# A routed feed-forward layer on one core: the second expert's search is written out earlier, and four weight pieces wait for a gather

## The chip, the core and the metric

The kernel runs on one core of a Trainium2 chip. Its engines work side by side, each through its own queue in order: TensorE (PE in the profile; its weight loads are PEld), VectorE (DVE), ScalarE (ACT), GpSimd (POOL) and SyncE (SP). SP issues the plain DMAs, POOL the indirect ones. The metric is the device time of one execution in microseconds (us). Before the change it was 879.24 us, the median of 3 runs (879.12 to 879.32).

## The reference

A retention layer (4 batches, 8 heads, 576 positions, head width 64) gives 2304 tokens of width 512. A dense feed-forward layer of width 2048 with its own activation follows. The last part is a routed layer over 8 experts:

```
logits = x @ w_gate                      # 2304 x 8
for idx in argsort(-logits.flatten()):   # best pairs first
    tok, e = idx // 8, idx % 8
    if assigned[tok] >= 0 or counts[e] >= 288: continue
    assigned[tok] = e; counts[e] += 1
for e in range(8):
    out[mask_e] = relu(x[mask_e] @ w1[e]) @ w2[e]   # 512 -> 1024 -> 512
```

Every expert takes exactly 288 tokens.

## The kernel before

`first_part` computes the retention layer and the dense layer and leaves the tokens in `ydram` and the logits in `L`. `second_part` does the routing and the experts.

**The search.** The greedy assignment is done in eight phases; each finds the expert that fills next and the logit at which it fills. For phases 0 to 6 the generator `routing_fast` runs three levels. At a level VectorE compares all logits with 63 or 64 thresholds (`reach`, L673), TensorE counts them per expert (18 small products, `cnt`, L955), VectorE marks the full ones (L959), TensorE adds the marks up (`dg`, L965) and VectorE makes the next, finer thresholds (`tau`, L971). After the third level (`de`, L975) a chain of small VectorE operations (L977 to L1004) gives the tokens of the phase (`sel`) and the number of the expert (`EINT`). `slots` (rp, L892) numbers the tokens; `compaction` turns these numbers into an index list `ix` by comparisons on VectorE (`hot`, L851) and 18 products on TensorE (`dv<-cv,hot`, L858). It puts its eight steps into the list `fills`. In the kernel before, `slots` follows at once only for phase 0 and the last two phases; for the others it waits in `pend` until the next phase's first count.

**The experts.** `fetch` issues the 512 KB pieces of an expert's weights on SP (L782), eight for each expert, into four buffers `wraw`; the first piece waits for `EINT`. `split` makes of each piece a rounded half `wxh` (ACT, L792) and a rest `wxl` (POOL or DVE, L794). Pieces 1 to 4 are the first layer, 5 to 8 the second. `gather` fetches the 288 rows by three indirect DMAs on POOL (L1195). `turn` and `transposes` turn them on TensorE (L1201), and ACT (L1214) and DVE (L1218) make the two halves `xth` and `xtl`. `ffn` is 192 products: 96 of the first layer (L1240) and 96 of the second (L1254); after each product it yields. `store` (L1265) turns the result back and scatters it during the next expert's products.

**What sets the order.** The order on each engine is the order in which the program writes it out. `clk` is a planner's clock for each engine, in estimated us. In the loop over an expert's products each product adds `MM` = 0.122 to `clk["pe"]`; between products the loop writes out the next step of the search (`step`, when `clk["route"]` is reached), the next step of a compaction (`fill`), the next expert's gather (as soon as its `ix` is written), a weight split, a store or a block of three turns. The generator's `yield cost, extra` tells how long VectorE is expected to need until the next step. If expert 1's index list is not there when expert 0's products are all written, the code below the loop forces the rest of the search and the gather before expert 1.

In the kernel before, the first count of phase 1 is written after 42 products of expert 0, its `slots` after 151, and its last compaction steps and gather only behind all 192. Expert 2's gather is written after 88 products of expert 1 and its first turns after 121.

**The start.** Ahead of the loop stand the whole search of phase 0, its first four pieces, its gather, one step of phase 1 (the comparisons of its first level, on DVE), the rests of the four pieces on DVE (`los`), the turns of expert 0 and then `fetch()`, which issues pieces 5 to 8; their buffers come free when `los` has read them.

Of the kernel before, what the change touches and what calls it, by code (L numbers as in the profile page):

```python
# [19 lines left out]
N, DM, FF, E, F = 2304, 512, 2048, 8, 1024  # L20
# [707 lines left out]
def second_part(ctx, tc, L, ydram, wx, cst, out, st, fast, L0=None):  # L728
# [5 lines left out]
    nc = tc.nc  # L734
# [38 lines left out]
    def fetch():  # L773

        while len(fetched) < 4 and SRC.get("next", 0) // 8 in EINT:
            n = SRC.get("next", 0)
            ph, i = n // 8, n % 8
            if i == 0:
                r = nc.sync.value_load(EINT[ph], min_val=0, max_val=E - 1)
                SRC[ph] = wx[bass.ds(r, 1)].rearrange("o p f -> p (o f)")  # L780
            raw = wk.tile([P, 1024], F32, tag="wraw", name="wraw", bufs=4)
            nc.sync.dma_start(raw, SRC[ph][:, i * 1024:(i + 1) * 1024])  # L782
            clk["dma"] = max(clk["dma"], clk["pe"] + 2.0) + 1.5
            fetched.append((ph, i, raw, clk["dma"]))
            SRC["next"] = n + 1
# [18 lines left out]
    clk = {"pe": 0.0, "dve": 0.0, "pool": 0.0, "route": 0.0, "dma": 0.0, "gather": 0.0}  # L804
# [3 lines left out]
    def on_dve(cost, ready=0.0):  # L808
        clk["dve"] = max(clk["dve"], clk["pe"], ready) + cost

    def rush(force=False):
        while urgent and (force or urgent[0][0] <= clk["pe"]):
            urgent.pop(0)[1]()
# [71 lines left out]
    def routing_fast():  # L885
# [3 lines left out]
        def slots(ph, sel, rs, dm=None):  # L889

            rp = ps_rt([P, 2], "rp")
            nc.tensor.matmul(rp[:, 0:1], tri, rs, start=True, stop=True, skip_group_check=True)  # L892
            nc.tensor.matmul(rp[:, 1:2], ones, rs, start=False, stop=True, skip_group_check=True)

            def rest():
                rps = rt([P, 2], "rps")
                V.tensor_copy(rps, rp)
                sl = sl_[ph % 2]
                V.tensor_tensor_scan(sl, one18, sel, rps[:, 0:1], op0=ALU.mult, op1=ALU.add)
                slot = rt([P, NT], "slot")  # L900
                V.tensor_mul(slot, sl, sel)
                compaction(ph, slot)

                def check():
                    V.scalar_tensor_tensor(bad, rps[:, 1:2], float(CAP), bad, op0=ALU.not_equal,
                                           op1=ALU.add)
                    if dm is not None:
                        V.scalar_tensor_tensor(bad, dm, 0.5, bad, op0=ALU.is_lt, op1=ALU.add)

                fills.append((None, check))  # L910

            return rest

        pend = None
        for ph in range(E):
# [88 lines left out]
            V.tensor_scalar(ei, em, -1.0, float(E), op0=ALU.mult, op1=ALU.add)  # L1004
            EINT[ph] = ei[0:1, 0:1]
            pend = (ph, sel, rs, dm)
            if ph == 0 or ph >= E - 2:
                yield 2.4, 0.06
                rest, pend = slots(*pend), None
                rest()  # L1010
                yield 1.2, 0.0
# [188 lines left out]
    def turn(tp, ph, k, kt):  # L1200
        nc.tensor.transpose(tp[:, k * 96:(k + 1) * 96], XG[ph][:, k, kt * P:(kt + 1) * P],  # L1201
                            identf[:96, :96])

    def transposes(ph, kt, tp=None):
        if kt == 0:
            XT[ph] = (wk.tile([P, KT, CAP], F32R, tag="xth", name="xth"),
                      wk.tile([P, KT, CAP], F32R, tag="xtl", name="xtl"))
        if tp is None:
            tp = psum.tile([P, CAP], F32, tag="tp", name="tp", bufs=2)
            clk["pe"] += 0.5  # L1210
            for k in range(3):
                turn(tp, ph, k, kt)
        xh, xl = XT[ph]
        nc.scalar.activation(xh[:, kt, :], tp, AF.Copy)  # L1214

        def rest():
            on_dve(0.4)
            V.tensor_sub(xl[:, kt, :], tp, xh[:, kt, :].bitcast(F32))  # L1218

        urgent.append((clk["pe"] + 0.6, rest))  # L1220
# [40 lines left out]
    def store(ph, k):  # L1261
# [21 lines left out]
        scat.append(st)  # L1283

    gen = routing_fast() if fast else routing()
    nxt_pe = [0.0]

    def step():

        clk["pe"] = max(clk["pe"], clk["route"]) + nxt_pe[0]  # L1290
        try:
            cost, nxt_pe[0] = next(gen)
            on_dve(cost, clk["pe"] + 0.25)
            clk["route"] = clk["dve"] + 0.15
        except StopIteration:
            clk["route"] = 1e9

    def pieces(ph, n):
        while len(WSET.get(ph, ())) < n:
            fetch()  # L1300
            split(eng=V if len(WSET.get(ph, ())) % 2 else None)

    while 0 not in EINT:
        step()
    fetch()
    los = [split(True) for i in range(4)]
    while not fills:
# [7 lines left out]
    los[3](V)  # L1315
    tps = [psum.tile([P, CAP], F32, tag=t, name="tp", bufs=b) for t, b in (("tp", 2), ("tp", 2), ("fp", 3), ("fp", 3))]
    for k in range(3):
        for kt in range(KT):
            turn(tps[kt], 0, k, kt)
    for kt in range(KT):  # L1320
        transposes(0, kt, tps[kt])
    rush(True)
    fetch()
    for ph in range(E):
        nxt = ph + 1 < E
# [56 lines left out]
def build(tc, ap, out):  # L1382
    nc = tc.nc
    with ExitStack() as ctx:
        pp = ctx.enter_context(tc.tile_pool(name="pp", bufs=1))
        dp = ctx.enter_context(tc.tile_pool(name="dp", bufs=1, space=bass.MemoryType.DRAM))
        cp = ctx.enter_context(tc.tile_pool(name="cp", bufs=1))
        ctx.enter_context(tc.manual_schedule())
        L = pp.tile([P, NT, E], F32, name="L")
        ydram = dp.tile([N, DM], F32, name="ydram")  # L1390
        cst = {}
        start = []
        cs = ExitStack()

        def begin():
            start.append(Search(cs, tc, L, cst))
            return start[0].early()

        with ExitStack() as c1:
            first_part(c1, tc, ap["att"], ap["att_ht"], ap["att_hn"], ap["dtab"], ap["qtab"],  # L1400
                       ap["ktab"], ap["stab"], ap["wi"], ap["wo"], ap["wgb"], ydram, L, lambda: constants(cp, tc, ap, cst), cst, begin, lambda *a: Grid(cs, tc, L, cst).pieces(*a))
        keep = ctx.enter_context(tc.tile_pool(name="keep", bufs=1, reuse_waits="tile"))
        L0 = keep.tile([P, NT, E], F32, name="L0")
        nc.gpsimd.tensor_copy(L0, L)
        with ExitStack() as c2:
            flag = second_part(c2, tc, L, ydram, ap["wx"], cst, out, start[0], True, L0)
            again = nc.values_load(flag[0:1, 0:1], min_val=0, max_val=1)
        cs.close()
        with tc.If(again != 0):
            with ExitStack() as c3:  # L1410
                general_constants(c3, tc, ap, cst)
                second_part(c3, tc, L0, ydram, ap["wx"], cst, out, Start(c3, tc, L0, cst), False)
# [91 lines left out]
```

## Time and profile before

| What | Number |
|---|---|
| median of 3 runs | 879.24 us |
| the profiled execution's own time | 882.06 us |
| its span, first to last instruction | 880.3 us |
| TensorE busy | 792.0 us, 90% of the span |
| VectorE busy | 574.8 us, 65% |
| POOL busy | 470.5 us, 53% |
| mean granted clock of TensorE | 0.942 |

A granted clock of 0.50 is TensorE's lower level, 1.2 GHz, and 1.00 the upper, 2.4 GHz. Times in rows count from the start of the span. A row of the timeline is: start, duration of the merged instructions, engine, line, operation, what is written from what, how many, and in brackets the idle time of the engine before it with what ended it.

### The profile page before, as it was taken

The numbers are of one execution on the slowest core, as the hardware profiler recorded it, in microseconds if no ns is written. First come the engines' busy times: TensorE is split into PE (matmuls) and PEld (weight loads), VectorE is DVE, ScalarE is ACT, GpSimd is POOL, SyncE is SP. The second block draws the span as 40 slices with busy tenths as digits, with TensorE's granted clock in tenths as the row PEclk, the third lists the DMA queues.
The fourth block names the chain that finished last, engine by engine and source line by source line (L and its number), as shares of the span: only waits on it lengthen the run. The fifth ranks groups of instructions, "written<-read, shape, count | busy, mean of one in ns | idle before, by whom it ended". The sixth has DMA issues, their size and how long they took to land.

```text
span 880.3 us, 16265 instructions
## 1 busy us (share of the span) xinstructions
PE 792.0 (90%) x6151; PEld 720.7 (82%) x6151; DVE 574.8 (65%) x1346; ACT 415.1 (47%) x891; POOL 470.5 (53%) x538
## 2 busy tenths in 40 slices
PE   6687788899999999999999989739699999999994
PEld 6676676788998889888888879629688899999993
DVE  4999999955555688797988955664656635532210
ACT  2454666654544454555455545223244444544621
POOL 3432222265544667566676645214367878778911
PEclk9798989999999999999999999859789999999997
DMA  8535343101204210211100000060546656556401
GB/s 315 178 110 173 125 128 119 50 25 49 68 29 144 73 49 25 96 49 42 65 16 25 2 25 1 25 218 1 172 147 184 181 175 196 149 161 209 124 29 31
DMA packets 27320, 87.63 MB, mean 100 GB/s; under 512 B 4448, under 2 KB 5600, under 8 KB 27104
## 3 DMA queue, kind: packets, MB, share of 16 engines
q1 hardware_dynamic: 24160, 77.06, 27.4%
q0 software_dynamic: 3072, 9.44, 3.3%
q8 instruction: 50, 0.82, 0.4%
q14 instruction: 38, 0.31, 0.1%
HBM read 77.05 MB, written 9.44 MB: 98 GB/s over the span
## 4 chain that ended last, share of the span: by engine, by line
PE 66%; DVE 20%; issue 6%; POOL 2%; DMA 2%; ACT 2%; SPq 0%; DVEq 0%; POOLq 0%; ACTq 0%
PE ph L311 19%; PE hp L1240 9%; PE op L1254 8%; PE b_E L398 8%; PE b_F L398 7%; DVE u L329 3%; DVE raw L162 2%; PE cnt L955 2%; DVE y L167 2%; PE b_A L218 1%; DVE raw L158 1%; DVE u L333 1%; DVE u L324 1%; DVE hot L851 1%; DMA xg<-ydram,ix 1%
## 5 line engine op out<-in xcount | busy, mean ns | idle before, releaser
L311 PE MATMUL ph<-xh,winh 128*128 128x256 f32 x576 | 166.5, 289 | 17.2 <-DVE u L339 11.8
L794 POOL TENSOR_TENSOR wxl<-wraw,wxh 128x1024 fp32r<-128x1024 f32 x58 | 137.6, 2394 | 56.5 <-ACT wxh L792 56.2
L311 PE MATMUL ph<-xl,winh 128*128 128x256 f32 x576 | 164.3, 285 | 0.0
L311 PE MATMUL ph<-xh,winl 128*128 128x256 f32 x576 | 164.2, 285 | 0.0
L329 DVE RECIPROCAL u<-u 128x128 f32<-128x128 f32 x144 | 137.0, 951 | 3.9
L346 POOL TENSOR_TENSOR gl<-u,gh 128x256 fp32r<-128x256 f32 x114 | 86.0, 754 | 93.5 <-ACT gh L345 92.7
L311 PEld LDWEIGHTS ph<-xh,winh 128*128 128x128 f32 x576 | 111.3, 193 | 28.8 <-DVE u L339 16.9
L320 ACT ACTIVATE d<-ph 128x256 f32<-128x256 f32 x144 | 54.9, 381 | 146.9 <-PE ph L311 130.2
L311 PEld LDWEIGHTS ph<-xh,winl 128*128 128x128 f32 x576 | 112.1, 195 | 4.9
L311 PEld LDWEIGHTS ph<-xl,winh 128*128 128x128 f32 x576 | 112.3, 195 | 0.2 <-DVE xl L254 0.2
L324 DVE TENSOR_TENSOR u<-d 128x128 f32<-128x128 f32 x144 | 56.4, 392 | 64.9 <-ACT d L322 59.5
L333 POOL TENSOR_TENSOR u<-d,u 128x128 f32<-128x128 f32 x112 | 52.4, 468 | 53.4 <-DVE u L329 53.3
L792 ACT ACTIVATE wxh<-wraw 128x1024 fp32r<-128x1024 f32 x64 | 67.0, 1052 | 20.1 <-DMA wraw<-in_wx_dram 20.1
L321 ACT ACTIVATE d<-d,half_b 128x256 f32<-128x256 f32 x144 | 73.4, 510 | 4.7
L334 POOL TENSOR_TENSOR u<-d,u 128x128 f32<-128x128 f32 x112 | 68.2, 609 | 8.8
L345 ACT ACTIVATE gh<-u 128x256 fp32r<-128x256 f32 x144 | 58.3, 405 | 17.4 <-DVE u L339 16.9
L322 ACT ACTIVATE d<-d 128x256 f32<-128x256 f32 x144 | 60.2, 418 | 4.5
L1231 DVE SCALAR_TENSOR_TENSOR htl<-hp,hth 128x288 fp32r<-128x288 f32 x64 | 28.7, 455 | 49.8 <-ACT hth L1243 46.8
L355 DVE SCALAR_TENSOR_TENSOR scr<-y,WG 128x512 bf16<-128x512 f32 x64 | 55.3, 864 | 0.4
L339 DVE SCALAR_TENSOR_TENSOR u<-u,ph 128x256 f32<-128x256 f32 x144 | 54.1, 376 | 0.3
L1240 PE MATMUL hp<-xth,wxh 128*128 128x288 f32 x256 | 51.8, 315 | 2.2 <-ACT wxh L792 1.2
L1243 ACT ACTIVATE hth<-hp 128x288 fp32r<-128x288 f32 x64 | 26.1, 408 | 54.5 <-PE hp L1240 48.9
(264 smaller groups left out, 1878.4 us busy)
## 6 DMA issues: line engine op xcount, KB each, us to landing
wraw<-in_wx_dram SPq DMA_DIRECT2D x64, 512.0 KB, 4.2
att<-in_att_dram SPq DMA_DIRECT2D x32, 512.0 KB, 5.4
raw<-in_wi_dram SPq DMA_DIRECT2D x16, 512.0 KB, 3.2
raw<-in_wo_dram SPq DMA_DIRECT2D x16, 512.0 KB, 3.4
ydram<-y SPq DMA_DIRECT2D x9, 512.0 KB, 2.8
WG<-in_wgb_dram SPq DMA_DIRECT2D x1, 2048.0 KB
att<-in_att_ht_dram SPq DMA_DIRECT2D x4, 256.0 KB, 3.7
att<-in_att_hn_dram SPq DMA_DIRECT2D x4, 256.0 KB, 4.2
```

Source lines behind the costliest of these rows:

```text
L311: nc.tensor.matmul(ph, w[f][:, kt, :], x[:, kt, :], start=(k == 0), stop=(k == 11))
L321: nc.scalar.activation(df, df, AF.Square, bias=half_b, scale=-0.5)
L324: nc.vector.tensor_mul(u[:, 0, :], d[:, 0, :], d[:, 1, :])
L329: nc.vector.reciprocal(r, r)
L333: eng.tensor_mul(u[:, 1, :], d[:, 0, :], u[:, 0, :])
L334: eng.tensor_mul(u[:, 0, :], d[:, 1, :], u[:, 0, :])
L346: eng.tensor_sub(gl, g, gh.bitcast(F32))
L398: nc.tensor.matmul(py[n][t], g[:, t * P:(t + 1) * P], w[f], start=(f == 0 and w is woh and g is gh), stop=(f == NF - 1 and g is gl))
L792: nc.scalar.activation(hi, raw, AF.Copy)
L794: rest = lambda eng: eng.tensor_sub(lo, raw, hi.bitcast(F32))
L1240: nc.tensor.matmul(hp, W[kt][w][:, s], x[:, kt, :], start=(k == 0), stop=(k == 11))
L1254: nc.tensor.matmul(op, W[4 + ft // 2][w][:, s], h[:, ft, :], start=(k == 0), stop=(k == 23))
```

## The change

Four edits. The fifth piece of all (`n == 4`) gets a one-column write on POOL ahead of its DMA, so that the DMA waits for POOL's queue, in which the first gather stands. Phase 1's `slots` follows at once, as phase 0's does. A `step()` (the counts of phase 1's first level) is written between the second and the third gathered block of expert 0's turns. A second `step()` (`dg`, `tau` and the comparisons of the second level) stands ahead of `fetch()`, and before it the planner's TensorE clock is set to VectorE's where that is later.

```diff
@@ -779,6 +779,9 @@
             raw = wk.tile([P, 1024], F32, tag="wraw", name="wraw", bufs=4)
+            if n == 4:
+
+                nc.gpsimd.memset(raw[:, 0:1], 0.0)
             nc.sync.dma_start(raw, SRC[ph][:, i * 1024:(i + 1) * 1024])
@@ -1004,7 +1007,7 @@
-            if ph == 0 or ph >= E - 2:
+            if ph < 2 or ph >= E - 2:
                 yield 2.4, 0.06
                 rest, pend = slots(*pend), None
                 rest()
@@ -1315,11 +1318,15 @@
     for k in range(3):
+        if k == 2:
+            step()
         for kt in range(KT):
             turn(tps[kt], 0, k, kt)
     for kt in range(KT):
         transposes(0, kt, tps[kt])
     rush(True)
+    clk["pe"] = max(clk["pe"], clk["dve"])
+    step()
     fetch()
```

## Rows read from the trace of the kernel before

**Rows 1.** Windows: busy us (instructions) of each engine, granted clock, DMA share, GB/s.

```profile
564.90:591.60 26.70, 8.20 (x89) 6.85 (x88) 17.19 (x52) 5.16 (x8) 3.47 (x3) 0.53 0.59 197
591.60:624.80 33.20, 33.18 (x274) 31.55 (x274) 17.66 (x59) 11.26 (x21) 13.06 (x6) 0.91 0.20 68
624.80:636.40 11.60, 5.88 (x68) 4.71 (x69) 8.12 (x31) 1.36 (x4) 3.92 (x4) 0.64 0.44 138
636.40:645.20 8.80, 7.26 (x28) 6.17 (x27) 3.92 (x4) 3.93 (x6) 3.81 (x2) 0.50 0.36 118
645.20:679.00 33.80, 32.21 (x290) 30.29 (x289) 21.20 (x74) 15.95 (x26) 24.89 (x18) 0.95 0.56 163
679.00:711.90 32.90, 31.08 (x289) 29.15 (x288) 18.63 (x64) 16.77 (x27) 28.39 (x20) 1.00 0.64 191
```

**Rows 2.** Page, part 6: the weight pieces' DMAs, count, size, median us from issue to landing.

```profile
wraw<-in_wx_dram SPq DMA_DIRECT2D x64, 512.0 KB, 4.2
```

**Rows 3.** Timeline, 581 to 593 us: the first gather, its turns, expert 0's first products.

```profile
581.02 1.63 POOL L1195 DMA_INDIRECT xg<-ydram,ix  x1 [16.60 <-DVE dv L908]
...
584.05 0.74 DVE L673 TENSOR_TENSOR ind<-dv,g_G 128x567 bf16<-128x567 f32 x1
584.18 0.92 POOL L1195 DMA_INDIRECT xg<-ydram,ix  x1 [0.30 <-issue]
...
586.27 0.87 PE L1201 MATMUL tp<-c_ident,xg 96*128 96x96 f32 x4 [6.53 <-DMA xg<-ydram,ix]
589.69 0.90 PE L1201 MATMUL tp<-c_ident,xg 96*128 96x96 f32 x4 [2.55 <-DMA xg<-ydram,ix]
590.76 0.90 PE L1201 MATMUL tp<-c_ident,xg 96*128 96x96 f32 x4 [0.17 <-DMA xg<-ydram,ix]
...
591.68 1.52 PE L1240 MATMUL hp<-xth,wxh 128*128 128x288 f32 x4
```

**Rows 4.** Windows: the four us in which the second and third blocks land.

```profile
586.00:590.00 4.00, 1.18 (x6) 0.92 (x7) 1.06 (x1) 0.00 (x0) 0.00 (x0) 0.50 0.99 291
```

**Rows 5.** Timeline, 630 to 635 us: the last block of expert 1's gather and its turns.

```profile
630.91 0.92 POOL L1195 DMA_INDIRECT xg<-ydram,ix  x1 [0.30 <-issue]
...
634.00 0.90 PE L1201 MATMUL tp<-c_ident,xg 96*128 96x96 f32 x4 [0.87 <-DMA xg<-ydram,ix]
```

**Rows 6.** Timeline, 637 to 642 us: expert 1's third and fourth weight pieces.

```profile
637.05 1.99 ACT L792 ACTIVATE wxh<-wraw 128x1024 fp32r<-128x1024 f32 x2
```

**Rows 7.** Timeline, 658 to 666 us: expert 2's gather and its first turns.

```profile
658.87 0.94 POOL L1195 DMA_INDIRECT xg<-ydram,ix  x1 [3.75 <-PE cnt L955]
...
665.27 0.30 PE L1201 MATMUL tp<-c_ident,xg 96*128 96x96 f32 x1 [1.08 <-DMA xg<-ydram,ix]
```

**Rows 8.** Windows: two stretches of products at the lower clock.

```profile
591.60:597.30 5.70, 5.68 (x23) 5.57 (x23) 2.01 (x5) 1.35 (x5) 0.00 (x0) 0.50 0.03 11
...
665.60:669.10 3.50, 3.36 (x14) 3.07 (x15) 2.08 (x12) 1.36 (x2) 2.86 (x2) 0.51 0.72 193
```

**Rows 9.** Timeline: products at the upper clock, a count, compaction products, a block of turns.

```profile
598.12 0.69 PE L1240 MATMUL hp<-xtl,wxh 128*128 128x288 f32 x4
598.64 0.69 PE L1240 MATMUL hp<-xth,wxl 128*128 128x288 f32 x4
...
600.07 0.75 PE L955 MATMUL cnt<-oh,ind 128*63 128x8 bf16 x18
...
656.00 0.39 PE L858 MATMUL dv<-cv,hot 128*96 128x6 bf16 x6 [0.35 <-DVE hot L851]
656.25 0.65 PE L1240 MATMUL hp<-xth,wxl 128*128 128x288 f32 x3
...
677.29 0.41 PE L1201 MATMUL tp<-c_ident,xg 96*128 96x96 f32 x3
677.49 0.65 PE L1254 MATMUL op<-hth,wxl 128*128 128x288 f32 x3
```

**Rows 10.** Timeline: a one-element write on POOL.

```profile
646.05 0.09 POOL L1277 MEMSET spacer<- 1x1 f32 x1
```

## The prediction

> **What bounds the kernel now.** I read the page's shares first: TensorE is busy 90% of the span, the next engine 65%, so what counts is where TensorE waits or runs slowly. Then I read the timeline from the end of the dense layer on, cut it into stretches by what TensorE does, and took busy time, granted clock and DMA for each from the windows [rows 1]. Five things are to be seen there:
>
> - From 564.9 to 591.6 us TensorE is busy 8.2 of 26.7 us: the search and compaction of phase 0 and the first gather, one after the other.
> - Expert 0 (591.6 to 624.8) has TensorE busy 33.18 of 33.20 us. Inside it nothing is waited for.
> - From 624.8 to 636.4 no product of an expert runs. TensorE is busy 5.9 of 11.6 us, with the last compaction steps of phase 1, expert 1's gather, and the search of phase 2. POOL and DMA are far from full.
> - Expert 1 takes 8.8 us at the lower clock for its first 22 products, then 33.8 us.
> - Expert 2, with the same kind of work between its products, takes 32.9 us, all at the upper clock.
>
> So the end is set by TensorE's order, and what can be won is the hole between experts 0 and 1 with the slow restart behind it, about 11.6 + 42.6 - 33 = 21 us, and a little at the first gather. Everything from expert 2 on is full: 31.1 of 32.9 us busy.
>
> **The pieces held back.** The first gather's last block leaves POOL at 584.18 + 0.92 = 585.10, and its turns start at 590.76, 5.66 us later [rows 3]. For expert 1 the same step is 631.83 to 634.00, 2.17 us [rows 5]. Between 586 and 590 all DMA engines are busy (0.99, 291 GB/s) [rows 4], and the only other traffic is pieces 5 to 8. With them behind POOL's third issue, block 3 can be there at 585.10 + 2.17 = 587.3, block 1 at 582.65 + 2.17 = 584.8, block 2 between them at about 586.0. The bounds are this (a gain of 3.5 us at the gather) and no gain, if the pieces still collide. I take the first: the pieces' DMAs leave SP about 585.3, and a piece takes 4.2 us to land [rows 2], while 512 KB at 291 GB/s [rows 4] are 1.8 us, so most of it passes before its bytes move.
>
> The write itself is 0.09 us [rows 10], at most the 0.92 us of an indirect issue; POOL has nothing behind it until expert 0's products run. On SP the three later pieces queue behind it and nothing else does. Piece 5 then lands at about 589.5; it is first read after 28 products, at about 595. That cover would have to shrink by 5 us to cost anything.
>
> **The first extra step.** The counts now stand on TensorE between the turns of blocks 2 and 3. Their comparisons are done at 584.79 [rows 3], so they start when block 2's turns end, at 586.0 + 0.9 = 586.9. At the upper clock a count takes at most 0.75 us [rows 9]; here, at the lower, twice 0.7, so 1.4: until 588.3. Block 3's turns, queued behind, start 1.0 us later than the data allow. The first product came 0.92 us after them [rows 3]; with `dg` in front of it I put 589.4. Gain 2.3 us; if the gather is no faster, a loss of 0.2 from `dg`. The second step's VectorE work (2 us) stands behind the four halves of `xtl` and ahead of the first rest of `ffn`, which frees one of three result buffers; no product waits for that before the fourth tile.
>
> **Where phase 1's steps go.** The planner's sums give the order. The step sets TensorE's clock to 23.52; four rests of 0.4 put VectorE at 25.52, to which the new line lifts TensorE; the second step makes that 25.57 and the next step due at 25.57 + 0.25 + 2.0 + 0.15 = 27.97. At 0.122 a product that is after 20 products. Carried on, the second count comes after 20 products, the third after 44, `EINT` after 49, `slots` after 72, compaction from 85, and expert 1's gather after 119; its turns after 161, 170, 179 and 189, and its first four weight splits after 137, 157, 167 and 178. So all that filled the hole is written before expert 0's products end.
>
> Expert 0, from its 33.2 us: one count and its `dg` leave (0.9) and one pair from phase 2 enters (0.9), together nothing. Three sets of compaction products at 0.25 each [rows 9] are +0.75, with waits for `hot` like the 0.35 there, +0.5. Four blocks of turns at 0.2 [rows 9] are +0.8. Gather 1 has 42 products at 0.13 [rows 9] and a count before its first turn, 6.2 us; it needs 0.8 to start, as expert 2's did, two issues of 1.24, then 0.92 + 2.17, so 6.4: +0.2. The lower clock lasted 5.7 us here [rows 8]; TensorE is now busy from 586.0 instead of 589.7 on, so it may rise up to 1.4 us earlier into the products, worth up to 0.7: -0.4. Sum 33.2 + 1.85 = 35.05; expert 1 starts at 624.5 instead of 636.4. Its weights: POOL, free of the gather 4.5 us after its start, needs four rests of 2.4 us and ends 14.1 us after it; TensorE wants the fourth 12.5 + 1.4 us after it. They meet.
>
> Expert 1, from 8.8 + 33.8 = 42.6 us: its first 22 products fall from 8.8 to 22 x 0.13 + 0.4 for the store = 3.3, -5.5. That holds the slow clock and the late splits [rows 6], both gone. Gather 2 stalled TensorE by 1.08 [rows 7], and the clock then fell: 14 products took 3.5 us instead of 1.8 [rows 8]. The stall came with a weight piece in flight; that split now comes earlier, to POOL, and POOL's order keeps the next piece behind the gather. It gets 31 products and two counts, 5.6 us, of the 6.4 it needs: 0.7 stays, without a fall (expert 2 idles 1.8 us at clock 1.00 [rows 1]); -2.1. The third count of phase 2, with `de`, moves in from the hole: +0.9. Sum 35.9; expert 2 starts at 660.4 instead of 679.0. From there the same work follows in nearly the same order, and from expert 3 on in the identical one.
>
> So the profiled execution would fall by 18.6 us, from 882.06 to 863.5. It lies 2.8 us above the median of the runs, so the forecast is 879.24 - 18.6 = **860.6 us**; 857.5 to 863 with the small waits at zero or doubled.
>
> **Rivals.**
>
> *The pieces still collide.* The new wait is for POOL's queue, not for the gather's data: block 3's issue ends 5.66 us before its turns [rows 3]. If the fifth piece starts as soon as POOL is free and takes the engines, block 3 lands as before. The first product then comes at 591.9, 2.5 us later than forecast: 863.1. For it speaks that the data trail the issue by 2.17 us even when little else moves [rows 5]; against it, that a piece's own start takes about as long. The Trainium skill ("Perfetto Trace Analysis", DMA Instruction — SWDGE (GPSIMD)) says that such an instruction's end in the profile is the end of descriptor generation and not of the data movement. The rows agree, 5.66 and 2.17 us; by that rule alone the sum would be this rival's.
>
> *The wait moves to the restart.* VectorE lags the planner, expert 1's gather or its third and fourth splits come late, TensorE stalls at the first turns, and the clock falls as for expert 2: 1.1 + 1.7 [rows 7, 8], and some 1.5 for late splits as at 637 [rows 6]. That is 4.3 us: 865. Against it, gather 1 has nine products more of room than gather 2 had.
>
> *Slower.* The counts now come 20 to 49 products into expert 0, while the clock is still low. If TensorE waits at them so often that the clock does not rise, each product costs 5.7/23 = 0.25 instead of 0.13. The whole gain is used up after 18.6/0.12 = 155 such products beyond the 23; with the other 169 of expert 0 it is 880.5. Against it: four counts stood in expert 0 before with 0.02 us of idle time [rows 1].
>
> *It doesn't do what it says.* VectorE is so late that TensorE waits in the loop for phase 1's index list as long as it did behind it: 879.
>
> **How the numbers follow.** Forecast 0.72, collision 0.14, late restart 0.09, no effect 0.02, slower 0.03. The range takes in the first two and most of the third: 857.5 to 866.0. A measurement of this kernel tells 0.2% (1.8 us) from no change; faster by more 0.95, within 0.02, slower 0.03.
>
> **What would show it.** Block 3's turns near 588.3 and expert 0's first product near 589.4; turns of expert 1 inside expert 0's products; no hole at 624; granted clock 1.00 from about 594 to the end of expert 2; expert 2's first product near 660. The forecast is wrong if TensorE idles over 2 us inside expert 0, or if the clock falls again before expert 2.

## The result, and the profile after

The changed kernel takes **863.63 us** (median; 862.65 to 863.90 in four executions), against 879.26 (879.12 to 879.32) for the kernel before in the same comparison: ratio 0.982 [0.9803, 0.9837], 15.6 us less. The forecast was 860.6 with a range of 857.5 to 866.0 and a gain of 18.6 us. The profiled execution of the changed kernel took 863.57 us (span 861.8); the sum made on the profile had put it at 863.5. Among the runs below, one execution of the kernel with slots as before took 990.51 us at a mean clock of 0.732 and is left out of that kernel's numbers.

Windows of the kernel after: bounds, length, then busy us (instructions) of TensorE, its weight loads, VectorE, ScalarE and POOL, granted clock, DMA share, GB/s. The stretches answer to [rows 1]: search and first gather, the first products of expert 0 at the lower clock, experts 0, 1 and 2.

```profile
564.90:589.20 24.30, 9.46 (x111) 8.05 (x108) 17.59 (x57) 5.58 (x8) 3.58 (x4) 0.54 0.49 162
589.20:594.40 5.20, 5.20 (x22) 4.98 (x21) 3.80 (x9) 1.29 (x4) 0.00 (x0) 0.52 0.72 269
589.20:624.40 35.20, 35.15 (x303) 33.33 (x303) 21.63 (x71) 14.35 (x26) 21.04 (x11) 0.93 0.47 149
624.40:660.90 36.50, 35.49 (x336) 33.28 (x335) 23.60 (x86) 17.48 (x30) 29.79 (x20) 1.00 0.61 180
660.90:694.80 33.90, 31.86 (x296) 30.18 (x296) 20.63 (x72) 17.41 (x30) 28.34 (x20) 1.00 0.61 186
```

There is no stretch without products between experts 0 and 1 any more: in [rows 1] 11.6 us lay there with TensorE busy 5.88. TensorE has 303 instructions in expert 0 where it had 274, and is idle for 0.05 us of it. Expert 1 starts at the upper clock.

The first gather in the timeline of the kernel after (start, busy us, engine, line, operation; in brackets what was waited for), which answers to [rows 3]:

```profile
584.54 0.92 POOL L1198 DMA_INDIRECT xg<-ydram,ix  x1 [0.30 <-issue]
585.26 0.87 PE L1204 MATMUL tp<-c_ident,xg 96*128 96x96 f32 x4 [5.17 <-DMA xg<-ydram,ix]
585.46 0.11 POOL L784 MEMSET wraw<- 128x1 f32 x1
...
586.42 0.90 PE L1204 MATMUL tp<-c_ident,xg 96*128 96x96 f32 x4 [0.29 <-DMA xg<-ydram,ix]
...
587.25 1.12 PE L958 MATMUL cnt<-oh,ind 128*63 128x8 bf16 x18
588.30 0.90 PE L1204 MATMUL tp<-c_ident,xg 96*128 96x96 f32 x4
...
589.14 0.18 PE L968 MATMUL dg<-cl,c_ones 63*128 63x1 bf16 x1
589.25 1.49 PE L1243 MATMUL hp<-xth,wxh 128*128 128x288 f32 x4
```

The third block's turns start 2.84 us after its issue ends (584.54 + 0.92 = 585.46) and wait for no DMA; before it was 5.66 with waits of 6.53, 2.55 and 0.17 ahead of the three blocks. The 18 products of the count stand ahead of the last block, as the sum had them; they took 1.12 us and not 1.4.

The starts of experts 1 and 2 in the same timeline, with the gathers that feed them; they answer to [rows 5] and [rows 7]:

```profile
612.22 0.93 POOL L1198 DMA_INDIRECT xg<-ydram,ix  x1 [3.87 <-PE op L1257]
...
617.50 0.61 PE L1204 MATMUL tp<-c_ident,xg 96*128 96x96 f32 x3
...
624.39 0.69 PE L1243 MATMUL hp<-xth,wxh 128*128 128x288 f32 x4
...
645.10 0.95 POOL L1198 DMA_INDIRECT xg<-ydram,ix  x1 [3.36 <-PE cnt L958]
...
650.64 0.30 PE L1204 MATMUL tp<-c_ident,xg 96*128 96x96 f32 x1 [0.18 <-DMA xg<-ydram,ix]
...
660.86 0.70 PE L1243 MATMUL hp<-xth,wxh 128*128 128x288 f32 x4
```

Expert 1's gather is issued 12 us before expert 0 ends, and its turns wait for nothing. Expert 2's stall is 0.18 us where it was 1.08.

### The profile page after: what moved, and what is told of

Read it like the earlier page. It is cut to its first block, busy times and chain, and to the rows that moved or that the text cites. A ratio compares the mean times of both kernels' runs of the same rounds, so it can differ in the third digit from the quotient of the medians.

```text
span 861.8 us, 16271 instructions
## 1 busy us (share of the span) xinstructions
PE 785.4 (91%) x6151; PEld 716.2 (83%) x6151; DVE 570.8 (66%) x1344; ACT 414.3 (48%) x891; POOL 475.5 (55%) x541
## 4 chain that ended last, share of the span: by engine, by line
PE 68%; DVE 19%; issue 6%; POOL 2%; ACT 2%; DMA 2%; SPq 0%; DVEq 0%; POOLq 0%; ACTq 0%
PE ph L311 19%; PE hp L1243 9%; PE op L1257 8%; PE b_E L398 8%; PE b_F L398 7%; DVE u L329 3%; DVE raw L162 2%; PE cnt L958 2%; DVE y L167 2%; PE b_A L218 1%; DVE raw L158 1%; DVE u L324 1%; DVE u L333 1%; PE b_E L433 1%; DVE gl L346 1%
## 5 line engine op out<-in xcount | busy, mean ns | idle before, releaser
L797 POOL TENSOR_TENSOR wxl<-wraw,wxh 128x1024 fp32r<-128x1024 f32 x60 | 142.4, 2396 | 30.9 <-ACT wxh L795 30.5
```

What stands on the lines that cost most here:

```text
L797: rest = lambda eng: eng.tensor_sub(lo, raw, hi.bitcast(F32))
```

## The experiments

The dense layer does not end at the same time in every execution (561.9 to 564.5 us in these records). So that only the changed part is compared, the table counts from the start of the dense layer's last copy to expert 0's, 1's and 2's first product and to the end of the span, in the one profiled execution of each kernel. The last column is the median of all executions, less the median of the kernel before in the same comparison. That one moves by itself: it was 879.26 beside the changed kernel, 880.03 beside its own repeat, no hold, slots at once and hold; 878.35 beside slots as before, no estimate line, the count behind block 3 and the first unread products; 880.27 beside the last two and the repeat of the changed kernel. So entries of one comparison can be set against each other, and entries of different ones only to about 2 us. The profiled execution is the slowest of its kernel for slots as before (870.71) and for the first unread products (868.03).

```
                              expert 0  expert 1  expert 2     end | medians
before                           29.77     74.50    117.11  318.39 |
kernel before, repeated          29.20     72.60    113.14  314.54 |  +0.5
changed kernel                   26.97     62.11     98.58  299.52 | -15.6
changed kernel, repeated         26.75     61.16     97.66  298.15 | -15.8
changed, no hold                 29.89     64.45    100.99  301.48 | -13.4
before + slots at once           28.90     68.53    113.35  316.88 |  +2.0
before + hold                    26.38     70.49    110.55  311.49 |  -1.7
changed, slots as before         26.93     67.86    107.55  304.74 | -11.4
changed, no estimate line        26.97     62.88     99.61  299.26 | -13.8
changed, count after block 3     27.53     63.28    100.00  298.85 | -14.4
changed + unread products        26.25     60.91    101.65  301.73 | -15.6
changed + more of them           28.75     66.20    102.75  303.11 | -11.5
the same, gather 2 later         29.18     66.14    102.24  303.12 | -14.1
```

**The two kernels again.** No edit; twelve more executions of the kernel before and five of the changed one.

> The kernel before, unchanged. Theory A: the profiled execution of before stood 2.8 us above its other runs because its second gather came late and the clock then fell (1.1 us of waiting, 1.7 us of slow products); an execution near 879.3 us shows the stretch 645.2 to 679.0 some 2.5 to 3 us shorter, with a granted clock of 1.00 in it. Rival B: that fall is in every execution and the 2.8 us lie elsewhere (first part, or the profiler's own cost); then a profile shows the same dip behind 665 us whatever its time.

> The changed kernel, unchanged, beside the two below and with more executions of before. Theory A (the forecast's base, the one profiled execution of before, was 2.9 us above an ordinary one in the part that the change touches): 15 to 16 us below the median of before, and, counted from the end of the dense layer, expert 0, 1 and 2 start within 0.7 us of the first profile of the changed kernel (27.0, 62.1, 98.6). Rival B: the changed kernel varies as before did, and its starts spread by 2 us or more.

Measured: the kernel before 880.54 (877.02 to 887.09, 12 executions; ratio to its own other executions 1.0013 [0.9993, 1.0033]); the changed kernel 864.52 (863.00 to 865.71), ratio 0.9823 [0.9802, 0.9843], again 15.75 us less. The starts of this second record lie within 0.2, 0.95 and 0.92 us of the first record, the latter two a little outside what was expected. The repeated record of the kernel before is the informative one. Its windows, with stretches like those of [rows 1] and expert 0's first 3.1 us on a line of their own:

```profile
591.00:594.10 3.10, 3.08 (x14) 3.00 (x14) 1.55 (x4) 0.91 (x4) 0.00 (x0) 0.54 0.08 32
591.00:622.90 31.90, 31.88 (x274) 30.28 (x274) 17.67 (x59) 11.24 (x21) 12.78 (x6) 0.96 0.20 70
622.90:634.40 11.50, 5.62 (x68) 4.44 (x69) 8.15 (x31) 1.33 (x4) 4.21 (x4) 0.72 0.47 142
634.40:643.10 8.70, 7.16 (x43) 6.07 (x42) 3.92 (x4) 4.46 (x7) 3.66 (x2) 0.59 0.35 120
643.10:675.00 31.90, 30.21 (x280) 28.49 (x277) 21.22 (x74) 15.48 (x26) 25.09 (x18) 1.00 0.60 175
675.00:708.90 33.90, 31.96 (x297) 30.21 (x296) 19.04 (x65) 17.61 (x29) 29.51 (x20) 1.00 0.63 189
```

The hole is the same, 11.5 us against 11.6 [rows 1]. But expert 0's clock rises after some 3 us instead of 5.7 [rows 8]; the first 8.7 us of expert 1 hold 43 instructions of TensorE at clock 0.59 where the 8.8 us of [rows 1] hold 28 at 0.50, so the clock rises earlier there too; and the rest of expert 1 runs at 1.00 throughout, 31.9 us instead of 33.8 (2.5 to 3 us less had been expected), although its stall is there:

```profile
662.63 0.30 PE L1201 MATMUL tp<-c_ident,xg 96*128 96x96 f32 x1 [1.17 <-DMA xg<-ydram,ix]
```

So the profile on which the sum was made holds 1.3 us in expert 0 and 2.1 us in expert 1 (42.6 against 40.5) that another execution of the same kernel does not have, and the stretches differ in the granted clock. The timed executions fit this: of 49 executions that stood beside the kernels below, six took over 882.06 us, and their mean clock was 0.939 to 0.941, near the 0.942 of the profiled one; the eleven of at most 878.2 us had 0.945 to 0.949.

**No hold.** The changed kernel without

```diff
-            if n == 4:
-
-                nc.gpsimd.memset(raw[:, 0:1], 0.0)
```

> The changed kernel without the one-column write, so that pieces 5 to 8 start as before. Theory A (the pieces delayed the first gather): block 3's turns near 590.8 instead of 588.3, expert 0's first product near 591.9, 2.5 us more than the changed kernel: about 866. Rival B (the first gather is slow by itself, the pieces don't matter): the same as the changed kernel, 863.6.

Measured 866.59 (865.02 to 868.61), 0.9847 [0.9822, 0.9872]: 3.0 us above the changed kernel's 863.63, or 2.2 by the last column of the table. The timeline of this run:

```profile
586.54 0.92 POOL L1195 DMA_INDIRECT xg<-ydram,ix  x1 [0.30 <-issue]
...
591.48 0.90 PE L1201 MATMUL tp<-c_ident,xg 96*128 96x96 f32 x4 [1.88 <-DMA xg<-ydram,ix]
```

Here the second block waits 1.88 us and starts 4.0 us behind the end of the third's issue; with the hold it started 0.96 behind. Everything after the first product is as in the changed kernel (34.56 us from expert 0 to expert 1, against 35.14 and 34.41). At the first product the hold is worth 2.9 us (3.1 against the repeat of the changed kernel) and by the medians 2 to 3 us, all at the gather.

**Hold alone.** The kernel before with those two lines.

> The kernel before with the one-column write alone. Theory A: block 3's turns at 587.3 instead of 590.8, and the whole rest moves by that: 3 to 3.5 us less than before, 876. Rival B (the gather is slow by itself): 879.3.

Measured 878.29 (876.36 to 883.02), 0.9983 [0.9965, 1.0001]. By the medians that is 1.7 us where 3 to 3.5 had been expected, and the interval reaches 1: not a difference by itself. Counted from the dense layer's end the first product comes 2.8 us earlier than in the repeat of the kernel before, and the end 3.1 us earlier. In its timeline the third block is clean, since no count stands ahead of it:

```profile
586.04 0.92 POOL L1198 DMA_INDIRECT xg<-ydram,ix  x1 [0.30 <-issue]
...
589.27 0.90 PE L1204 MATMUL tp<-c_ident,xg 96*128 96x96 f32 x4 [0.44 <-DMA xg<-ydram,ix]
590.19 1.52 PE L1243 MATMUL hp<-xth,wxh 128*128 128x288 f32 x4
```

The turns start 589.27 - 586.96 = 2.31 us behind the issue's end, where the forecast took 2.17 and the kernel before had 5.66 [rows 3].

**Slots at once alone.** The kernel before with

```diff
-            if ph == 0 or ph >= E - 2:
+            if ph < 2 or ph >= E - 2:
```

> The kernel before with the second phase's slots at once, and nothing else. By the planner's sums gather 1 is then written after 168 products of expert 0, and all of its turns behind product 192. Theory A: of the 6.4 us that the gather needs, 24 products and the rest cover 3.2; the hole of 11.6 us shrinks to 3 to 4 us, expert 0 starts as in before (591.7): 868 to 870, 872 if the clock falls in the hole. Rival B (the search, not the place of slots, makes the hole): within 2 us of before.

Measured 882.05 (876.97 to 884.03), 1.0021 [1.0002, 1.004]. A plain miss: no gain where 10 us and more had been expected. Its windows (experts 0 and 1, each to the next one's first product):

```profile
592.70:632.30 39.60, 35.31 (x281) 32.89 (x282) 17.87 (x58) 12.54 (x24) 17.01 (x9) 0.89 0.29 90
632.30:677.10 44.80, 41.02 (x351) 37.07 (x350) 23.91 (x75) 17.65 (x30) 26.71 (x18) 0.88 0.41 131
```

And its timeline:

```profile
624.28 0.92 POOL L1195 DMA_INDIRECT xg<-ydram,ix  x1
...
628.80 0.91 PE L1201 MATMUL tp<-c_ident,xg 96*128 96x96 f32 x2 [3.05 <-DMA xg<-ydram,ix]
...
632.35 0.83 PE L1240 MATMUL hp<-xth,wxh 128*128 128x288 f32 x2
...
669.33 0.95 POOL L1195 DMA_INDIRECT xg<-ydram,ix  x1 [4.61 <-PE cnt L955]
...
674.54 0.96 PE L1201 MATMUL tp<-c_ident,xg 96*128 96x96 f32 x5 [0.51 <-DMA xg<-ydram,ix]
...
678.69 1.16 PE L1240 MATMUL hp<-xtl,wxh 128*128 128x288 f32 x4
```

The hole between experts 0 and 1 shrinks (39.6 us from start to start instead of 43.4 in the repeat of the kernel before), but the next search is written later: expert 2's gather goes out at 669 us, 37 us into expert 1 where it was 22.5 before (658.87 [rows 7] less 636.4 [rows 1]), its turns come behind expert 1's last products, and expert 2 starts at the lower clock (1.16 us for four products where 0.7 is usual). Expert 1 takes 44.8 us, against 42.6 and 40.5 in the two records of the kernel before. The hole is handed on to the next expert.

**Slots as before.** The changed kernel with the old condition, `ph == 0 or ph >= E - 2`: hold, estimate and early steps alone.

> The changed kernel with the second phase's slots left for the next phase's first count, as before; the two earlier steps and the held pieces stay. By the planner's sums gather 1 is then written after 150 products of expert 0 (119 in the changed kernel, behind 192 in before) and its first turns after 181. Theory A (what matters is how many products lie between a gather and its turns; the earlier steps alone pull it inside expert 0): 31 products and two counts are 5.6 us of the 6.4 needed, expert 1 starts 1 us later than in the changed kernel, 864 to 865.5. Rival B (slots at once closes the hole): the hole comes back, 870 or more.

Measured 866.97 (866.24 to 870.71, five executions), ratio 0.9859 [0.9835, 0.9882]: 3.3 us above the changed kernel's 863.63, or 4.2 by the last column, between the two theories. The timeline of this run at expert 1's start, in its slowest execution:

```profile
621.31 0.93 POOL L1198 DMA_INDIRECT xg<-ydram,ix  x1 [3.65 <-PE cnt L958]
...
630.60 0.81 DVE L1221 TENSOR_TENSOR xtl<-tp,xth 128x288 fp32r<-128x288 f32 x2
631.09 1.22 PE L1204 MATMUL tp<-c_ident,xg 96*128 96x96 f32 x6 [2.12 <-DVE xtl L1221]
632.02 1.40 PE L1243 MATMUL hp<-xth,wxh 128*128 128x288 f32 x4
```

And its windows there:

```profile
630.00:635.00 5.00, 3.91 (x18) 3.83 (x19) 2.32 (x6) 1.77 (x3) 3.31 (x2) 0.58 0.67 204
635.00:640.00 5.00, 5.00 (x37) 4.50 (x35) 1.04 (x6) 0.61 (x2) 1.18 (x2) 0.50 0.41 126
```

Gather 1 is issued 9 us later than in the changed kernel (7 counted from the dense layer's end), its last turns fall behind expert 0's products, TensorE waits 2.12 us for VectorE there, and the clock goes to 0.50. That is the forecast's second rival, the wait moved to the restart, at its place and at about its price of 4.3 us; in the changed kernel the early slots keep it away. The hold and the early steps without the early slots still keep 11.4 of the 15.6 us.

**Estimate and place of the count.** Two pieces taken out of the changed kernel, one in each run:

```diff
-    clk["pe"] = max(clk["pe"], clk["dve"])
```

```diff
-        if k == 2:
-            step()
```

> The changed kernel without the line that lifts the planner's TensorE clock to VectorE's. The second count then comes after 30 products instead of 20 and gather 1 after 126 instead of 119, its turns after 168. Theory A: everything still lies inside expert 0, within 1 us of the changed kernel, 863 to 864.6. Rival B (the spacing is what makes it): VectorE is still the late one at 20 products in the changed kernel, so ten products more save waits, or the later gather costs 2 us or more: outside 862 to 866.

> The changed kernel without the step between the second and third gathered block; the first level's counts stand behind all turns, ahead of expert 0's first product. Theory A: block 3's turns move up from 588.3 to the landing at 587.5, the counts (1.1 us at the lower clock) then stand ahead of the first product, which moves from 589.25 to 589.5: within 0.7 us of the changed kernel. Rival B (the counts fill TensorE's wait and bring the upper clock forward): 1.5 us or more above it, 865.2.

Measured 864.55 (863.59 to 864.65), 0.9825 [0.9803, 0.9847], and 863.94 (862.54 to 864.66), 0.9821 [0.9798, 0.9843]. Neither differs from the changed kernel by more than its own two medians, 863.63 and 864.52, do; the last column, 13.8 and 14.4 us, cannot tell them from it either. Without the extra step the timeline shows the third block at 589.09:

```profile
589.09 0.90 PE L1204 MATMUL tp<-c_ident,xg 96*128 96x96 f32 x4 [0.51 <-DMA xg<-ydram,ix]
```

That is 3.28 us behind the start of its issue, against 3.76 in the changed kernel: the count holds the last turns up by 0.5 us, and spares as much afterwards (expert 0 starts at 26.97 us in the changed kernel and at 27.53 without the step). No run has the early steps alone, or hold and slots without any early step; what the steps give is known only as the difference between the changed kernel and the parts above.

**Filling the gaps with unread products.** To raise the clock before expert 0, the changed kernel gets products that nobody reads (`warm(n)` writes n of them, 128x128 by 128): in the first run 7 behind the products of `slots` and 14 behind those of the compaction, in the second more of them, from the search on.

```diff
     while not fills:
         step()
+    warm(7)
     fill(True)
+    warm(14)
```

> The changed kernel with products that nobody reads in TensorE's two waits ahead of expert 0: 7 of 128x128 by 128 float32 behind the rp products and 14 behind the compaction products (some 0.42 us each at the lower clock). Theory A (expert 0's first 20 products pay for the idle time ahead of them): the clock is up when block 1 lands, the counts and turns take half, and the first 20 products 0.13 instead of 0.25 us: 2.5 to 3.5 us less than the changed kernel, 860 to 861. Rival B: the clock does not rise in these waits or falls again at once, and expert 0 starts at the lower clock: 863.6, or up to 1 us more where the products run past the landing.

> The changed kernel with unread float32 products (128x128 by 128) in every wait of TensorE during the search of phase 0 and the first gather: 3 behind each dg, 7 behind de, 13 behind rp, 20 behind the compaction products. Theory A (an idle TensorE ahead of expert 0 costs the lower clock in the counts, the turns and the first 20 products): if they hold the upper clock that expert 1 to 7 have, each count on the way takes 0.7 instead of 1.3 us and expert 0's first 20 products 2.6 instead of 5 us: 3 to 4.5 us below the changed kernel, 859 to 860.5. Rival B (as when 21 such products in two waits raised the clock only near the end and it fell again): the unread products run at the lower clock, 0.42 us each, and stand in the way of the counts: 863 to 866.

> The same, and the planner takes gather 2 to need 1 us more, so that expert 2's first turns come after 142 of expert 1's products instead of 134. Theory A (the stall at expert 2's first turns and the fall of the clock behind it come in some executions and cost up to 3 us there): the median is 0.2 to 1 us below the kernel with unread products alone, and no profile shows the lower clock inside expert 1. Rival B: the turns, now 15 products apart, wait for VectorE instead; the same or up to 1 us more.

The third run is the second with 1 us more for gather 2 in the planner's estimate, so that expert 2's turns are written later. Measured: 862.80 (861.10 to 868.03), 0.9803 [0.9781, 0.9825], 0.8 below the changed kernel, within the spread and not below it in the last column; 868.80 (866.97 to 869.47), 0.987 [0.9846, 0.9894]; 866.21 (863.31 to 867.47), 0.983 [0.9805, 0.9854]. Windows of the first of them around expert 0's start, in its slowest execution:

```profile
590.00:592.00 2.00, 1.85 (x9) 1.41 (x10) 1.30 (x4) 1.32 (x4) 0.00 (x0) 0.81 1.02 342
592.00:594.00 2.00, 2.00 (x10) 2.00 (x10) 1.97 (x5) 0.00 (x0) 0.00 (x0) 0.50 0.97 385
```

And of the second:

```profile
580.00:585.00 5.00, 4.70 (x49) 4.70 (x49) 4.08 (x10) 3.23 (x4) 2.45 (x2) 1.00 0.52 193
585.00:590.00 5.00, 2.30 (x31) 1.72 (x29) 3.41 (x7) 0.00 (x0) 1.14 (x3) 1.00 0.76 226
590.00:595.00 5.00, 4.82 (x24) 4.58 (x25) 3.58 (x9) 1.73 (x5) 0.00 (x0) 0.66 0.78 297
```

The unread products do bring TensorE to its upper level, but it does not stay there: in both runs it falls to the lower one just as expert 0's products begin. In the second TensorE was busy for only 2.30 of the 5 us before. There the third block is late as well, and inside expert 0 a turn of expert 1 waits, as the timeline shows:

```profile
585.41 0.92 POOL L1210 DMA_INDIRECT xg<-ydram,ix  x1 [0.31 <-issue]
...
590.03 0.55 PE L1216 MATMUL tp<-c_ident,xg 96*128 96x96 f32 x4 [1.52 <-DMA xg<-ydram,ix]
...
620.20 0.30 PE L1216 MATMUL tp<-c_ident,xg 96*128 96x96 f32 x1 [1.42 <-DMA xg<-ydram,ix]
```

The block's turns start 3.70 us behind the issue's end, in the third run 4.03, against 2.31 with the hold alone. The wait inside expert 0 is 1.42 us, in the third run 1.23; behind it the granted clock is 0.58 from 621 to 624.5 us in both, and expert 0 takes 37.45 and 36.96 us, against 35.14 and 34.41 in the two records of the changed kernel. Why the two gathers are late there is open. The third run's median lies 2.6 us below the second's, yet their profiled executions end alike (303.1), so the runs do not show what the later turns are worth. None of the three is clearly better than the changed kernel, and the second is worse.

## Why the prediction was right, and 3 us too low

**The time and the rivals.** 863.63 us lies outside the 857.5 to 863 that the forecast gave for its own mechanism, and 0.5 us from the 863.1 of the rival with the colliding pieces. It lies in the full range only because that takes in two rivals, and neither of them happened; so the range held by luck, and the mechanism has to be read from the trace.

**Hold at the gather: right.** The forecast put block 3's turns at 588.3 and expert 0's first product at 589.4; they came at 588.30 and 589.25. Counted from the dense layer that is 2.8 us earlier than before (2.3 forecast). The two runs that add or remove the hold alone confirm mechanism and size at the first product: 2.8 and 2.9 us. By the medians, removing it costs 2 to 3 us and adding it gives 1.7, which is not clear of the spread. The pieces still come; they come behind the rows. In the 1.5 us behind the third issue the DMA share is 0.67, against 0.89 in the kernel before; from 586 to 590 it is 0.95, against 0.99 [rows 4]. The rival of the colliding pieces is out for the changed kernel, though not for every kernel with the hold: in two of those with unread products the third block was late.

**No hole, and a restart at the upper clock: right.** The order came as worked out: the second and third count stand behind 20 and 44 products of expert 0. Expert 0 was forecast at 35.05 us and took 35.14 (34.41 in the repeat); expert 1 at 35.9 and took 36.47 (36.50). Gather 2 kept 0.18 us of the 0.7 forecast. The late restart and the slow clock inside expert 0 did not come, and the change as a whole was not without effect, though the estimate line and the place of the count are when taken alone. That the early slots give nothing without the early steps, while steps and hold keep most of the gain without the slots, was not in the forecast: it worked out both from the planner's sums without asking what each would do alone.

**The step that failed: the base.** "It lies 2.8 us above the median of the runs, so the forecast is 879.24 - 18.6 = **860.6 us**". The 18.6 were a difference to one execution, and they were taken from the median as if the excess of 2.8 us lay outside the changed part. Most of it lay inside. The two records of the kernel before differ by 3.8 us: 0.6 ahead of expert 0's first product, 1.3 in expert 0, 2.1 in expert 1, and -0.1 behind. The change against either record:

```
us                            forecast   first records   repeated records
to expert 0's first product       -2.3            -2.8               -2.5
expert 0 to expert 1              -9.7            -9.6               -9.0
expert 1 to expert 2              -6.7            -6.1               -4.0
the rest                             0            -0.3               -0.9
```

Against its own profile every stretch came within 0.6 us, and the execution within 0.1. Against the second record of the kernel before, expert 1 gives 4.0. The mis-sized terms are these:

- The -2.1 at gather 2, in which the clock's fall counts 1.7 [rows 7, 8]. From the stalled turn to expert 2's first product the first record has 679.02 - 665.27 = 13.75 us and the second, with a stall of 1.17 us but clock 1.00, 675.00 - 662.63 = 12.37. So 1.4 us of it are lost in one execution and not in the other.
- The -5.5 at the restart. From expert 1's first product to that turn the first record has 28.86 us and the second 28.17: 0.7 us.
- Expert 0's 33.2 us, from which its gain is counted, held 1.3 us of late rise. The changed kernel's expert 0 varies by 0.7 itself (35.14 and 34.41), which leaves 0.6.

The term -0.4 for a clock that rises earlier is borne out by no run. In the kernel before it rose 5.7 and some 3 us into expert 0, in the changed kernel some 5 and some 3.5: two executions of one kernel differ by more than the term, and that the sum for expert 0 came out within 0.1 us is luck in this part.

What the change can save of a loss that only some executions have is its mean, not the profile's. Had the profile's gain less its 2.8 us of excess been taken from the median, 879.2 - 15.8 = 863.4 would have stood there. The records show the excess in one execution and its absence in another; how often the fall came in the executions that were only timed is not recorded, beyond their mean clocks.

All these terms took the slow products of one record for a property of the kernel. Expert 0 began with 5.7 us at the lower clock [rows 8] in one execution and with some 3 in the other; of two stalls of 1.08 and 1.17 us at the same place one was followed by the lower clock and one was not. The Trainium skill ("TensorE: Matmul & The Clock Gate", What's actually happening) says that the same kernel shows different counts of slow products at its start from run to run, and advises against fitting to one count. These two records show the same in the middle of a kernel.

## What to carry to other kernels

Before a gain worked out on a profile is subtracted from a median, ask where that profile's excess over the median lies: if in the stretch that is changed, it is part of the gain and must be counted once. A search that is written earlier for one expert has to be early for the one after it as well, or the hole only moves; so look one round further than the edit. A transfer that others wait for can be put ahead of bulk loads by making the loads depend on a cheap write queued behind its issue: 0.11 us here bought 2 to 3.

## What the runs showed that was not expected

- Stalls of TensorE at the turns of a gather had different ends. 1.08 us before expert 2 was followed by the lower clock [rows 8], 1.17 us in the repeat was not, nor 0.71 us with the hold alone; 1.68 us in the first run with unread products was, and so were 1.42 and 1.23 us before expert 1 in the other two. Windows of the first run with unread products, up to the end of the stall and behind it, 0.97 for five us, then 0.50 for four:

```profile
648.00:653.00 5.00, 3.48 (x39) 3.12 (x37) 1.15 (x5) 1.36 (x2) 4.67 (x4) 0.97 0.43 119
653.00:657.00 4.00, 3.84 (x16) 3.58 (x17) 2.73 (x14) 0.93 (x3) 1.21 (x1) 0.50 0.81 241
```

- The clock can fall with hardly a wait ahead of it: in the first run with unread products it was 1.00 from 588 to 590 us with TensorE busy for 1.78 of the 2 us, 0.81 in the next two (1.85 busy) and 0.50 in the two after (2.00 busy).
- The kernel before spreads over 877.1 to 883.3 us in 49 executions, its mean clock over 0.939 to 0.950 (in the twelve of the repeat, up to 887.1 at 0.935); the changed one over 862.65 to 865.71 in nine.
